# Agent attention and a squared-ReLU layer on one core: the step table that spaces the softmax chains of two query groups

## The chip, the cores and the metric

The kernel runs on one core of a Trainium2 chip. The metric is the device time of one execution in microseconds (us); the lower, the better. The kernel before was timed in three runs, with a median of 1907.89 us (1907.49 to 1918.07).

## The reference

Four batches of 12480 queries, keys and values of 128 channels, and 49 agents. The agents attend to the keys (`agent_v`), the queries attend to the agents, and the 49920 rows that come out go through a layer with a hidden width of 2048, all in float32:

```python
a2k = sm(agents, k)
agent_v = a2k @ v
q2a = sm(q, agents)
x = (q2a @ agent_v).reshape(B * S, D)
h = x @ w_in
r = np.maximum(h, 0.0)
return (r * r) @ w_out
```

`sm` is a softmax over scores scaled by 1/sqrt(128), with the maximum taken off.

## The kernel before

Since `agent_v` has only 49 rows, the kernel folds it into the weights of the layer: for each batch it makes `agent_v @ w_in` (49 x 2048) and multiplies the softmax of the queries, 49 wide, with it.

The query rows are cut into 49 groups of 1024. A group takes 16 *steps* of the main loop (784 in all), each for 512 rows and two of the 16 hidden blocks. Step i issues `mm1(i)` (6 matmuls at L440 into a PSUM tile `h`, of which there are two), `relu(i)` (ScalarE, L446, reads `h`), on every second step `square` (ScalarE, L449), `high` and `low` (VectorE, L453 and L457: the value split into two parts for fp32r matmuls), and `mm2` of a step 5 earlier (12 matmuls at L468 into one of two PSUM tiles `pair`). So mm1(i+2) needs relu(i) to have read its `h`. After 8 steps of mm2 `store` copies the sum out (ScalarE L473, VectorE L474) and writes 256 KB of the output (L475).

Beside this runs, for each group s, a chain that makes its softmax and lays it out with the 49 agents on the partitions:

- `q_load` (L313, 512 KB), then `q_scores` (matmuls L179) and `q_shift` (VectorE L333, L334, into buffer `e`), for two groups at once
- `q_exp` (ScalarE L337), `q_inverse` (VectorE L341 to L346), `q_norm` (GpSimd L349), `q_hi` (ScalarE L359) and `q_lo` (GpSimd L362), which leave `pp`, the softmax as two parts
- `q_turn` (L381): one transposing DMA from `pp` into `turned`, as 16-bit halves. Here it is called the *transpose*
- `q_sort` (L387): four DMAs that bring the lower and the upper halves into the two `planes`. The *sorts*
- `q_weave` (L392): two copies that put the halves together again in `woven`, one on ScalarE and one on GpSimd. The *joins*
- `q_spread` (L399): three DMAs, 1 MB in all, into `p_a` and `p_b`, which mm1 reads

There is one `pp` and one `planes`; `turned`, `woven` and the loaded tiles take turns in nine buffers. All DMAs are issued by SyncE's queue (SP), in program order: one that waits holds up those behind it. For the next batch a second chain runs: keys are loaded and scored (`k_load`, `k_scores`), the maximum is taken off (`k_sub`, GpSimd L214), `k_exp` (ScalarE L217), `v_load` and `v_acc` (matmuls L229).

The order on each engine is the program's. It comes from a list of (step, function) pairs, sorted by the step (L701): a fractional step number only sets the place in the order, nothing waits for a clock. `chain` (L494) finds for a row of functions the next free places on ScalarE, VectorE and TensorE. `plan_tokens(s, base)` (L531) calls it for one group; for an even s it also places the scores of s and s+1, and starts the softmax of s three steps behind them:

```python
first, base = chain(base, [("PE", q_scores, s, m), ("DVE", q_shift, s, m)])
...
base += 3
```

Of the kernel before, what the change touches and what calls it, by code (L numbers as in the profile page):

```python
# [25 lines left out]
def agent_attention_relu2_kernel(ctx: ExitStack, tc: tile.TileContext, qT, kT, v, agT, w_in, w_out, outT):  # L26
# [6 lines left out]
    nc = tc.nc  # L33
# [7 lines left out]
    NF = F // P  # L41
# [436 lines left out]
    LAG = 5  # L478
    steps = []

    def at(t, f, *args):
        steps.append((t, len(steps), f, args))
# [11 lines left out]
    def chain(t, todo):  # L494

        first = prev = None
        while todo:
            n = 1  # L500
            while todo[0][0] == "PE" and n < len(todo) and todo[n][1] in reads_bank and todo[n][0] != "PE":
                n += 1
            t += hop[prev][todo[0][0]] if prev else 0
            while True:
                g, p, ts = t, None, []
                for e, *_ in todo[:n]:
                    g += hop[p][e] if p else 0
                    while (e, g) in taken or (e == "PE" and g not in slots):
                        if p == "PE" and e == "DVE":
                            break  # L510
                        g += 1
                    ts.append(g)
                    p = e
                if todo[0][0] != "PE" or ts[-1] <= ts[0] + 1:
                    break
                t += 1
            for (e, f, *args), g in zip(todo, ts):
                soon = e == "DVE" and prev == "PE"
                if soon:
                    read.add(g)  # L520
                else:
                    taken.add((e, g))
                at(g + (.49 if soon and f is q_shift else .47 if soon else .45 if e == "PE" else .5), f, *args)
                prev = e
            first = ts[0] if first is None else first
            t, todo = ts[-1], todo[n:]
        return first, t
# [3 lines left out]
    def plan_tokens(s, base):  # L531
        todo = [("ACT", q_exp, s), ("DVE", q_inverse, s), ("POOL", q_norm, s), ("ACT", q_hi, s)]
        todo += [("POOL", q_lo, s)] + ([("PE", q_transpose, s), ("ACT", q_copy, s)] if s < 3 else [])
        if s > 1 and s % 2 == 0:
            m = min(2, NSG - s)
            first, base = chain(base, [("PE", q_scores, s, m), ("DVE", q_shift, s, m)])
            for x in range(s, s + m):
                at(first - 5, q_load, x)
            base += 3
        _, end = chain(base, todo)  # L540
        if s > 2:
            at(end + 1.9, q_turn, s)
            at(end + 3.9, q_sort, s)
            _, end = chain(end + 6, [("ACT", q_weave, s, 1, nc.scalar.copy)])
            at(end + .6, q_weave, s, 0, nc.gpsimd.tensor_copy)
        at(max(end + .9, (s - 1) * NF + .9), q_spread, s)
        assert end + 3 < s * NF, (s, end)

    def plan_batch(b, base):
# [128 lines left out]
    for y, x in enumerate((1.15, 1.16, 1.17)):  # L678
        at(x, w_first, 0, 4, 4, y, nc.vector)
    at(3.1, warm_rows, 6)  # L680
    plan_tokens(1, 3)
    for s in range(2, NSG):
        plan_tokens(s, (s - 2) * NF + NF // 2 + LAG - (0 if s < 3 else 8 if s % 2 else 3))
    t = 0
    for b in range(1, B):
        t = plan_batch(b, t)
# [41 lines left out]
```

## Time and profile before

| | us |
|---|---|
| median of three runs | 1907.89 |
| the profiled execution | 1912.69 |
| its span, first to last instruction | 1910.9 |
| TensorE busy | 1847.5 (97%) |
| ScalarE busy | 1676.3 (88%) |
| VectorE busy | 1670.2 (87%) |
| GpSimd busy | 388.3 (20%) |
| mean granted clock of TensorE | 0.989 |

The span leaves 1.8 us of the profiled execution outside. Engines in the rows: PE is TensorE's matmuls, PEld its weight loads, DVE VectorE, ACT ScalarE, POOL GpSimd, SP SyncE (SPq its queue of DMA issues). Busy time of PE overlaps from matmul to matmul, so a busy PE is not one at its full rate.

### The profile page before, as it was taken

The page shows a single profiled execution, that of the slowest core. Times are in us where ns is not written, and L with a number is a line of the kernel's source. Part 1 is how long each engine was busy: PE and PEld are TensorE (multiplying, and loading weights), DVE is VectorE, ACT ScalarE, POOL GpSimd, SP SyncE. Part 2 cuts the span into 40 slices and gives each one's busy share as a digit, 9 for nine tenths or more (in the row PEclk, how much of TensorE's full clock was granted, in tenths as well). Part 3 has the DMA queues.
Part 4 walks back from the last instruction along what each step waited for, and adds up shares of the span by engine and source line. Part 5 has one row for each costly group of instructions (what it writes and reads, how often), then busy time and mean ns, then how long its engine had stood idle before and what let it go on. Part 6 is the DMA issues. An engine that isn't in the chain of part 4 may idle for free.

```text
span 1910.9 us, 51820 instructions
## 1 busy us (share of the span) xinstructions
PE 1847.5 (97%) x23244; PEld 1482.4 (78%) x23244; DVE 1670.2 (87%) x1274; ACT 1676.3 (88%) x1535; POOL 388.3 (20%) x199
## 2 busy tenths in 40 slices
PE   9999999999999999999999999999999999999999
PEld 8688777787787877877788778777777787787787
DVE  7789897899888979989888899898888898898898
ACT  5788888898888979989888898899888998999997
POOL 1111232220201304213021142131220310210200
PEclk9999999999999999999999999999999999999999
DMA  9334432534434234244352342433522323323320
GB/s 383 111 90 126 121 88 92 139 87 145 127 102 122 75 105 118 82 120 115 116 156 82 97 113 82 120 101 92 143 65 71 95 77 86 95 64 99 95 70 21
DMA packets 158192, 204.75 MB, mean 107 GB/s; under 512 B 103408, under 2 KB 103664, under 8 KB 157970
## 3 DMA queue, kind: packets, MB, share of 16 engines
q1 hardware_dynamic: 157970, 201.44, 36.4%
q8 instruction: 182, 2.98, 0.6%
q14 instruction: 40, 0.33, 0.1%
HBM read 83.02 MB, written 25.56 MB: 57 GB/s over the span
## 4 chain that ended last, share of the span: by engine, by line
PE 50%; DMA 17%; ACT 11%; issue 7%; POOL 6%; DVE 5%; SPq 4%; ACTq 0%; POOLq 0%; DVEq 0%
PE pair L468 29%; PE h L440 16%; DMA turned<-pp 10%; ACT rg L446 6%; DMA planes<-turned 5%; SPq L387 3%; POOL pp L362 3%; PE pair L179 3%; ACT woven L392 2%; DVE gl L457 2%; POOL woven L392 2%; ACT rg L449 1%; DVE gh L453 1%; PE pair L229 1%; SPq L399 1%
## 5 line engine op out<-in xcount | busy, mean ns | idle before, releaser
L457 DVE TENSOR_TENSOR gl<-rg,gh 128x2048 fp32r<-128x2048 f32 x392 | 942.8, 2405 | 19.6 <-DVE gh L453 0.5
L446 ACT ACTIVATE rg<-h 128x1024 f32<-128x1024 f32 (+1 forms) x784 | 789.2, 1017 | 111.9 <-PE h L440 111.3
L449 ACT ACTIVATE rg<-rg 128x2048 f32<-128x2048 f32 x392 | 749.3, 1911 | 9.2
L453 DVE CAST gh<-rg 128x2048 fp32r<-128x2048 f32 x392 | 496.4, 1266 | 162.4 <-ACT rg L449 154.2
L468 PE MATMUL pair<-gh,wo_hi 64*128 64x512 f32 x3136 | 631.4, 393 | 1.5 <-issue 1.5
L468 PE MATMUL pair<-gh,wo_lo 64*128 64x512 f32 x3136 | 631.5, 393 | 0.0
L440 PE MATMUL h<-p_a,w_hi 49*128 49x512 f32 (+4 forms) x1616 | 509.6, 396 | 48.9 <-ACT rg L446 48.1
L440 PE MATMUL h<-p_b,w_hi 49*128 49x512 f32 (+4 forms) x1616 | 512.6, 396 | 1.7 <-DMA p_b<-w_lo 1.7
L468 PE MATMUL pair<-gl,wo_hi 64*128 64x512 f32 x3136 | 500.8, 393 | 1.8 <-DVE gl L457 1.7
L440 PEld LDWEIGHTS h<-p_a,w_hi 49*128 49x128 f32 x1616 | 287.0, 187 | 113.8 <-ACT rg L446 74.6
L468 PEld LDWEIGHTS pair<-gh,wo_lo 64*128 64x128 f32 x3136 | 310.6, 187 | 68.7
L468 PEld LDWEIGHTS pair<-gh,wo_hi 64*128 64x128 f32 x3136 | 309.1, 186 | 69.0 <-issue 1.7
L468 PEld LDWEIGHTS pair<-gl,wo_hi 64*128 64x128 f32 x3136 | 301.4, 185 | 72.2 <-DVE gl L457 6.9
L440 PE MATMUL h<-p_a,w_lo 49*128 49x512 f32 (+4 forms) x808 | 314.7, 389 | 0.0
L440 PE MATMUL h<-p_b,w_lo 49*128 49x512 f32 (+4 forms) x808 | 314.7, 389 | 0.0
L440 PEld LDWEIGHTS h<-p_b,w_hi 49*128 49x128 f32 x1616 | 289.6, 187 | 27.9 <-DMA p_b<-w_lo 2.0
L349 POOL TENSOR_TENSOR e<-e,sm 128x392 f32<-128x392 f32 x48 | 78.3, 1631 | 1020.6 <-DVE sm L346 906.6
L392 POOL COPY woven<-planes 128x1024 uint16<-128x1024 uint16 x46 | 125.8, 2735 | 253.8 <-DMA planes<-turned 189.4
L440 PEld LDWEIGHTS h<-p_a,w_lo 49*128 49x128 f32 x808 | 150.1, 186 | 29.0
L440 PEld LDWEIGHTS h<-p_b,w_lo 49*128 49x128 f32 x808 | 150.1, 186 | 1.7
L392 ACT COPY woven<-planes 128x1024 uint16<-128x1024 uint16 x46 | 62.8, 1366 | 75.1 <-DMA planes<-turned 65.5
L362 POOL TENSOR_TENSOR pp<-e,pp 128x392 fp32r<-128x392 f32 x48 | 99.4, 2071 | 114.5 <-ACT pp L359 114.5
(109 smaller groups left out, 858.9 us busy)
## 6 DMA issues: line engine op xcount, KB each, us to landing
vt<-v SPq DMA_DIRECT2D x52, 516.0 KB
qt<-qT SPq DMA_DIRECT2D x49, 512.0 KB
kt<-kT SPq DMA_DIRECT2D x52, 480.0 KB
outT<-ob SPq DMA_DIRECT2D x97, 256.0 KB
p_b<-woven SPq DMA_DIRECT2D x92, 256.0 KB
p_a<-woven SPq DMA_DIRECT2D x46, 512.0 KB
planes<-turned SPq DMA_DIRECT2D x184, 98.0 KB
raw<-w_in SPq DMA_DIRECT2D x4, 512.0 KB
```

Source lines behind the costliest of these rows:

```text
L179: nc.tensor.matmul(ps[r, u, c * A:(c + 1) * A], x[:, c, r], ag_sb[:, batch(c, r), :], start=True, stop=True)
L229: nc.tensor.matmul(ps[r], vt[:CH, c, r], piece(x)[:, c, :], start=x == n and c == 0, stop=x == n + m - 1 and c == G - 1)
L349: eng.tensor_tensor(out=es[s], in0=es[s], in1=sms.pop(s).to_broadcast([P, G, A]), op=ALU.mult)
L362: eng.tensor_tensor(out=halves(s)[1], in0=es.pop(s), in1=halves(s)[0].bitcast(F32), op=ALU.subtract)
L387: nc.sync.dma_start(out=to, in_=pss["t", s][w:2 * A:2, x])
L392: copy(PT["x"][:, :, :, w], planes[:, w])
L440: nc.tensor.matmul(h[:, u, x0:x1], w[ra[u], j, :], pt[u ^ lo][ra[u], x0:x1], start=x == 0, stop=x == 2)
L446: nc.scalar.activation(rgs[p][:, x], hs.pop(i)[:, :, :width(i)], AF.Relu)
L449: nc.scalar.activation(rgs[p], rgs[p], AF.Square)
L453: nc.vector.tensor_copy(ghs[p], rgs[p])
L457: nc.vector.tensor_tensor(out=gls[p], in0=rgs.pop(p), in1=ghs[p].bitcast(F32), op=ALU.subtract)
L468: nc.tensor.matmul(outs[t][u][:, :width(i)], w[rg[u], 2 * j + e, :], g[rg[u], e, :], start=j == 0 and x == 0, stop=j == NJ - 1 and x == 5)
```

## The change

Three numbers of the plan are moved.

```diff
         if s > 2:
-            at(end + 1.9, q_turn, s)
-            at(end + 3.9, q_sort, s)
-            _, end = chain(end + 6, [("ACT", q_weave, s, 1, nc.scalar.copy)])
+            at(end + 2.4, q_turn, s)
+            at(end + 4.9, q_sort, s)
+            _, end = chain(end + 8, [("ACT", q_weave, s, 1, nc.scalar.copy)])
             at(end + .6, q_weave, s, 0, nc.gpsimd.tensor_copy)
-        at(max(end + .9, (s - 1) * NF + .9), q_spread, s)
+        at(max(end + 1.4, (s - 1) * NF + .9) if s > 2 else end + .9, q_spread, s)
...
     for s in range(2, NSG):
-        plan_tokens(s, (s - 2) * NF + NF // 2 + LAG - (0 if s < 3 else 8 if s % 2 else 3))
+        plan_tokens(s, (s - 2) * NF + (13 if s < 3 else 7 if s % 2 else 6))
```

The places that come out are the same for all groups from 4 on (an odd group 3 too), in steps counted from step 16(s-2); an odd group's count begins 16 steps behind that of its even partner, and group s is first read at 32:

| | exp | norm | hi, lo | transpose | sorts | joins | spread |
|---|---|---|---|---|---|---|---|
| even s, before | 13.5 | 14.5 | 16.5 | 17.9 | 19.9 | 22.5 | 22.9 |
| even s, after | 9.5 | 10.5 | 13.5 | 15.4 | 17.9 | 21.5 | 22.4 |
| odd s, before | 5.5 | 6.5 | 8.5 | 9.9 | 11.9 | 14.5 | 16.9 |
| odd s, after | 7.5 | 8.5 | 10.5 | 12.4 | 14.9 | 18.5 | 19.4 |

The scores of a pair go from 10.45 to 6.45 of the even group's count. Stores stand at 4.2 and 12.2 of every 16. Some loads and matmuls of the key and value chain find other places a few steps away, since the places that they took are taken or free.

On SP's queue, from the transpose of group 16 to the load of groups 18 and 19, before (`turned<-pp` is a transpose, `planes<-turned` the sorts, `p_a` and `p_b<-woven` the spread, `outT<-ob` a store, `vt<-v` a load of values, `qt<-qT` one of queries):

```order
L381 DMA_TRANSPOSE turned_8943<-pp_90 128x16x128
L387 DMA planes_92<-turned_8943 49x1024 x4
L475 DMA outT<-ob_9014 128x512
L399 DMA p_b_9076<-woven_9071 64x1024 x2
L399 DMA p_a_9075<-woven_9071 128x1024
L221 DMA vt_9129<-v 128x1032
L221 DMA vt_9131<-v 128x1032
L381 DMA_TRANSPOSE turned_9159<-pp_90 128x16x128
L387 DMA planes_92<-turned_9159 49x1024 x4
L475 DMA outT<-ob_9231 128x512
L399 DMA p_b_9399<-woven_9348 64x1024 x2
L399 DMA p_a_9398<-woven_9348 128x1024
```

and the same place now:

```order
L381 DMA_TRANSPOSE turned_8890<-pp_90 128x16x128
L387 DMA planes_92<-turned_8890 49x1024 x4
L475 DMA outT<-ob_9014 128x512
L399 DMA p_b_9070<-woven_9040 64x1024 x2
L399 DMA p_a_9069<-woven_9040 128x1024
L221 DMA vt_9127<-v 128x1032
L221 DMA vt_9129<-v 128x1032
L475 DMA outT<-ob_9225 128x512
L381 DMA_TRANSPOSE turned_9231<-pp_90 128x16x128
L387 DMA planes_92<-turned_9231 49x1024 x4
L313 DMA qt_9395<-qT 128x1024
L313 DMA qt_9397<-qT 128x1024
```

The odd group's transpose (the second in each) stands right behind a store now, where it stood ahead of it, and the next pair's query loads stand right behind its sorts, ahead of its spread.

On GpSimd, from the first part of group 17's softmax (L349) to the joins of 16 and 17 (L392), before (`sk` at L214 is the key chain's k_sub, `pp` at L362 is q_lo):

```order
L349 TENSOR_TENSOR e_91<-e_91,sm_9041 128x392
L392 COPY woven_9071<-planes_92 128x1024
L214 TENSOR_TENSOR sk_99<-sk_99,mM_106 120x392
L362 TENSOR_TENSOR pp_90<-e_91,pp_90 128x8x49
L392 COPY woven_9348<-planes_92 128x1024
```

and now:

```order
L392 COPY woven_9040<-planes_92 128x1024
L214 TENSOR_TENSOR sk_99<-sk_99,mM_106 120x392
L349 TENSOR_TENSOR e_91<-e_91,sm_9095 128x392
L362 TENSOR_TENSOR pp_90<-e_91,pp_90 128x8x49
L214 TENSOR_TENSOR sk_99<-sk_99,mM_106 120x392
L392 COPY woven_9445<-planes_92 128x1024
```

Group 16's join stood between the two GpSimd operations of group 17's softmax; now it stands ahead of both.

## Rows read from the trace of the kernel before

**Rows 1.** Who waited for whom: us in total, times, longest us.

```profile
ACT woven L392 <- DMA planes<-turned: 65.5, 26, 7.3
PE h L440 <- ACT rg L446: 48.1, 44, 3.4
```

**Rows 2.** Timeline of ACT around the join of group 17: start us, us, instruction, idle before.

```profile
672.44 1.01 ACT L446 ACTIVATE rg<-h 128x1024 f32<-128x1024 f32 x1
679.31 1.34 ACT L392 COPY woven<-planes 128x1024 uint16<-128x1024 uint16 x1 [5.85 <-DMA planes<-turned]
```

**Rows 3.** Timeline of PE: the first matmul of steps 252, 254 and 257.

```profile
665.46 0.49 PE L440 MATMUL h<-p_a,w_hi 49*128 49x512 f32 x1 [0.40 <-ACT rg L446]
...
669.76 0.39 PE L440 MATMUL h<-p_a,w_hi 49*128 49x512 f32 x1
...
681.58 0.79 PE L440 MATMUL h<-p_a,w_hi 49*128 49x512 f32 x1 [3.41 <-ACT rg L446]
```

**Rows 4.** The chain that ended last, PE pieces: start us, us, what.

```profile
627.20 1.52 PE pair L179 x128
...
683.23 2.56 PE pair L468 x12
...
692.94 0.71 PE h L440 x6
693.65 1.40 PE pair L468 x12
```

**Rows 5.** Stretches: length, busy us (instructions) of PE, PEld, DVE, ACT, POOL, PEclk, DMA, GB/s.

```profile
602.00:612.00 10.00, 8.84 (x53) 7.07 (x55) 7.02 (x6) 8.91 (x9) 0.00 (x0) 0.66 0.38 105
...
1805.00:1812.00 7.00, 5.67 (x36) 4.57 (x38) 3.52 (x2) 6.94 (x7) 0.38 (x1) 0.76 0.55 152
```

**Rows 6.** Stretches: three periods of 32 steps in the last batch, and 60 us without a stall.

```profile
1573.83:1791.15 217.32, 209.92 (x2116) 167.04 (x2114) 192.92 (x133) 198.99 (x175) 34.97 (x18) 0.99 0.32 85
...
1595.00:1655.00 60.00, 60.00 (x630) 48.23 (x630) 56.75 (x41) 57.11 (x52) 9.32 (x5) 1.00 0.30 74
```

**Rows 7.** Timeline of POOL from group 17's norm to its q_lo.

```profile
655.21 1.65 POOL L349 TENSOR_TENSOR e<-e,sm 128x392 f32<-128x392 f32 x1 [10.68 <-ACT rg L446]
656.80 3.43 POOL L392 COPY woven<-planes 128x1024 uint16<-128x1024 uint16 x1
660.15 1.98 POOL L214 TENSOR_TENSOR sk<-sk,mM 120x392 f32<-120x392 f32 x1
662.09 3.00 POOL L362 TENSOR_TENSOR pp<-e,pp 128x392 fp32r<-128x392 f32 x1
```

**Rows 8.** Timeline of SP's issues, the same stretch: the us are those of the issue.

```profile
660.26 1.18 SPq L399 DMA_DIRECT2D p_b<-woven  x2
...
662.11 2.26 SPq L221 DMA_DIRECT2D vt<-v  x2
665.12 4.98 SPq L381 DMA_TRANSPOSE turned<-pp  x1
673.54 3.07 SPq L387 DMA_DIRECT2D planes<-turned  x4
676.72 0.39 SPq L475 DMA_DIRECT2D outT<-ob  x1
```

**Rows 9.** The chain that ended last, group 14's transfers: start us, us, what.

```profile
568.36 4.29 DMA turned<-pp
...
575.05 3.44 DMA planes<-turned
```

**Rows 10.** The same view, the last sort of group 13.

```profile
516.99 4.30 DMA planes<-turned
```

**Rows 11.** Timeline of SP, the issues behind group 13's sorts.

```profile
517.79 0.40 SPq L475 DMA_DIRECT2D outT<-ob  x1
518.24 1.11 SPq L174 DMA_DIRECT2D kt<-kT  x2
```

**Rows 12.** Timeline of DVE: the addition of the store at step 252.

```profile
670.10 0.68 DVE L474 TENSOR_TENSOR ob<-ob,pair 128x512 f32<-128x512 f32 x1
```

## The prediction

> **What bounds the kernel now.** I read the waits first, then the timeline of one long wait, then the stretches by engine.
>
> The waits name one pair [rows 1]: ScalarE stood 65.5 us at its joining copy because the sorts had not landed, and TensorE stood 48.1 us at mm1 because a relu came late. The timeline shows that these are one thing. ScalarE finishes a relu at 673.45 and begins the join at 679.31, after 5.85 us of waiting [rows 2]. The relus behind it in ScalarE's order are late by as much, mm1 has two `h` tiles and soon lacks a free one, and step 257 waits 3.41 us [rows 3]. So a wait on ScalarE reached TensorE with about 0.6 to 0.7 of its length (3.41/5.85, 48.1/65.5).
>
> A long wait costs twice. In the undisturbed stretch 6 matmuls of mm1 take 0.71 and 12 of mm2 1.40 us, 2.10 for a step; behind the stall the same 12 take 2.56 [rows 4]. [...] There are seven such stretches. (1 - clock) x length is 3.4 us in two of them (0.34 x 10) and 1.7 in five (0.24 x 7): 15.3 us.
>
> Without a stall TensorE is busy for all of 60 us and ScalarE for 57.1 of them [rows 6]. So TensorE bounds the kernel and ScalarE has 5% to spare: little, but it keeps pace there.
>
> The losses thus add up to 48.1 + 15.3 = 63.4 us. Idle time undercounts, since ends of matmuls are modelled; three whole periods show by how much. 96 steps between the transposes of groups 41 and 47 took 217.32 us; 96 x 2.10 plus three pairs of scores at 1.52 [rows 4] make 206.2, so 11.1 were lost, where idle time (217.32 - 209.92 = 7.4) and one clock stretch (1.7) tell 9.1 [rows 6]. At that ratio, 1.22, the whole is 77 us. I take 70 as what there is to win.
>
> Why the joins wait is in GpSimd's and SP's order, shown best at group 17. Its norm (655.21) is ahead of group 16's join, which runs from 656.80 and delays group 17's q_lo to 662.09 + 3.00 = 665.09 [rows 7]. The spread of group 16 can go only after that join, at 660.26, two value loads follow at 662.11, and the transpose of 17 is issued at 665.12 behind 2 MB of them: its sorts start 8.4 us later [rows 8], against 4.3 for a transpose with nothing ahead [rows 9].
>
> **The change part by part.** No instruction is added or removed; all durations stay. What changes is the distance between a chain's links, in steps of 2.10 us.
>
> *Distance from q_lo to the join:* six steps before, eight now, in every group: 4.2 us more for the transfers. They need, from the transpose's issue, 4.29 to its landing, 2.4 for the first three sorts, 3.44 for the last to land [rows 9]: 10.1 us. The longest single wait was 7.3 us [rows 1], so distance alone leaves at most 3.1 of it.
>
> *Even groups:* q_lo stands at step 13.5. It needs q_hi, which ScalarE reaches 3.7 us or less after the step's start, and takes 2 to 3 us [rows 7]: I take 5.5 to 6.5 us after the start of step 13. The halves then lie ready at 15.6 to 16.6 us. ScalarE comes to the join 3.7 us after the start of the join's step (673.45 against step 254 at 669.76 [rows 2, 3]), here 8 x 2.10 + 3.7 = 20.5. Four us are spare: no wait.
>
> *Odd groups:* on GpSimd the even join now goes ahead of the odd norm, and the even spread and the loads are issued some six steps (12.6 us) before the odd transpose instead of 3 to 5 us. So the 8.4 us should fall to 4.3. But the odd transpose is now behind the store of step 12. SP must wait for that addition: 670.10 + 0.68 against step 252's start at 665.46, 5.3 us [rows 12, 3], which is later than q_lo (step 10, 4.2 us earlier, plus 6). Then 10.1 us of transfers, and one more price: the next pair's query loads (1 MB) are issued right behind the sorts. Group 13 had a store and key loads there [rows 11], and its last sort took 4.30 instead of 3.44 [rows 10, 9]: 0.9. Ready at 5.3 + 10.1 + 0.9 = 16.3 us after step 12's start. ScalarE comes to the join at step 18: 6 x 2.10 + 3.7 = 16.3 us. The spare time is nil where TensorE has nothing extra in these six steps (15 of the 23 odd groups), and 1.5 us where a key score or `v_acc` lies in them (8). With an error of 0.8 us either way, those 15 wait about 0.45 us on average, 0.7 of which arrives at TensorE: 5 us in all, and too short to bring the clock down.
>
> *The store itself* puts 256 KB into the same DMA queue just ahead of the transpose. The trace has no such pair. From one side it costs nothing (no gain, as it adds work); from the other, 2 MB ahead cost 8.4 - 4.3 = 4.1 us [rows 8, 9]. I take an eighth, 0.5, by bytes: it lies inside the error above; 4.1 is kept for the range.
>
> [...]
>
> *The scores' move* to step 6.45 puts them two steps behind a store that empties the same PSUM tile. The store's addition ends 5.3 us after step 4's start; TensorE comes to the scores after the third step, 6.3. One us is spare. Their query loads, now behind the odd sorts, leave SP 5.3 + 4.3 + 3.1 = 12.7 us after the odd step 12 and are wanted at step 22, 21 us: they have 8 us to land.
>
> *Lost cover:* an earlier spread or a later one costs nothing; group s is first read at step 32 and the latest spread is at 22.4.
>
> The sum: 70 of losses less 5 that stay makes 65. Against its own time that is 1912.7 - 65 = 1848 for a profiled execution; the median of the runs shown lies 4.8 lower, so 1907.9 - 65 = **1843 us**.
>
> **The rivals.**
>
> *The odd waits stay (A).* If the store costs the transpose the full 4.1 us, ScalarE waits 16.3 + 4.1 - 16.3, about 4 us, in 15 odd groups and 2.5 in 8: 80 us, of which 0.7 or 56 reach TensorE, with little clock loss. Then 1907.9 - 70 + 56 = 1894. For it: zero spare time and the order on SP. Against: bytes.
>
> *ScalarE becomes the bound (B).* Without stalls there is no point at which lateness is wiped out, and ScalarE has 2.9 us spare in 60 [rows 6]. At the joins it gets 1.34 (join), then a store copy and an exponential within two to three steps. If each of 46 joins costs TensorE 0.5 us, 23 us stay: 1866. Against: the even joins stood as close to a store before, most without a wait.
>
> *GpSimd stands in front of the odd softmax (C), slower.* Place: the even join, now ahead of the odd norm, blocks GpSimd until the even sorts have landed; q_hi on ScalarE waits for the norm. The join should end near 16.6 + 3.4 = 20 us after the start of the even step 13, a k_sub behind it at 22, and the norm is wanted when the odd scores' sums are there, 11 steps and 3 us (26 us) after it; q_hi has 2 more. It decides from 6 us of lateness on; group 17's transpose was 4.1 us late. To eat 65 us, each of 23 odd groups must be late by 6 us and cost TensorE 3 us beyond that: 1907.9 - 65 + 69 = 1912 or above. Nothing in the rows shows even transfers so late.
>
> *It does nothing (D).* The waits move with the join, because the later transpose eats the distance in both kinds of group: 1900 to 1908. The even groups' four spare us speak against it.
>
> **How the numbers follow.** Forecast 0.73, A 0.11, B 0.08, D 0.04, C 0.04. The forecast's own range is 1907.9 - 77 = 1831 to 1858 (losses 63, 13 left). With B and half of A the range is 1829 to 1876. About 1% (19 us) is what a measurement of this kernel can tell from no change; faster by more than that (under 1889) are the forecast, B and about half of A, 0.90; within it D and some of A, 0.06; slower 0.04.
>
> **What would show it right or wrong.** Right: ScalarE's wait for the sorts falls from 65.5 us to under 10, TensorE's for the relu from 48.1 to under 10; the mean granted clock rises from 0.989 to about 0.997, since (1 - 0.989) x 1910.9 = 21 us, of which 15.3 go; odd transposes take 4 to 5 us, and SP holds them for the store's addition and no longer for q_lo. A shows as odd transposes of 6 us and more with joins that wait. B shows as waits of TensorE for relus with no wait of ScalarE ahead. C shows as waits of q_hi (L359) on GpSimd. The forecast is wrong if the joins no longer wait and the time still stays over 1876.

## The result, and the profile after

The changed kernel takes 1850.59 us (median of four runs, 1849.86 to 1854.21), the kernel before 1909.66 beside it (four runs, 1907.49 to 1918.07). The ratio is 0.9687, with a 95% interval of 0.9654 to 0.9719: 59 us less, of a forecast 65. The predicted 1843.0 is 7.6 us too low, and the range of 1829 to 1876 holds the result.

The waits of after, all engines, that answer to [rows 1] (us in total, times, longest us):

```profile
ACT woven L392 <- DMA planes<-turned: 5.9, 6, 1.8
...
ACT woven L392 <- issue: 4.8, 5, 1.8
...
PE pair L179 <- issue: 4.2, 2, 3.6
...
PE h L440 <- ACT rg L446: 3.6, 7, 0.8
...
PE pair L468 <- issue: 2.9, 2, 2.5
...
PE pair L229 <- issue: 1.8, 3, 0.9
```

Before, ScalarE waited 75.1 us at the joins: 65.5 put down to the sorts [rows 1] and 9.6 with nothing named. Now the same two rows of L392 make 10.7. TensorE's waits for relus fell from 48.1 us [rows 1] to 3.6. The three "issue" rows of PE are what the prediction doesn't have: TensorE stood 8.9 us with nothing in the profile to wait for (here and below, single waits of 0.2 us and less are left out). In the kernel before there were two such rows, 1.5 us each; they stand here behind its "issue" row of the joins:

```profile
ACT woven L392 <- issue: 9.6, 5, 4.4
...
PE pair L468 <- issue: 1.5, 1, 1.5
PE pair L229 <- issue: 1.5, 1, 1.5
```

Span and granted clock of after; before it was 1910.9 us at 0.989:

```profile
core 0: 1852.4 us, clock 0.996
```

The chain that ended last, by engine, of before and then of after (share of the span):

```profile
PE 50%; DMA 17%; ACT 11%; issue 7%; POOL 6%; DVE 5%; SPq 4%; ACTq 0%; POOLq 0%; DVEq 0%
```

```profile
PE 77%; DVE 7%; ACT 6%; issue 5%; DMA 4%; SPq 1%; POOL 0%; ACTq 0%; DVEq 0%; POOLq 0%
```

The transfers and GpSimd, 23% of the chain together, are down to 4%: the joins no longer hold the end.

Group 17 once more, the place of [rows 7, 8]. Timeline of SP (start us, us of the issue):

```profile
636.67 1.17 SPq L399 DMA_DIRECT2D p_b<-woven  x2
...
638.55 2.32 SPq L221 DMA_DIRECT2D vt<-v  x2
654.00 0.34 SPq L475 DMA_DIRECT2D outT<-ob  x1
654.44 2.23 SPq L381 DMA_TRANSPOSE turned<-pp  x1
660.12 3.07 SPq L387 DMA_DIRECT2D planes<-turned  x4
663.23 0.93 SPq L313 DMA_DIRECT2D qt<-qT  x2
```

Timeline of GpSimd, the same stretch:

```profile
630.89 3.10 POOL L392 COPY woven<-planes 128x1024 uint16<-128x1024 uint16 x1 [5.50 <-DMA planes<-turned]
...
643.01 1.66 POOL L349 TENSOR_TENSOR e<-e,sm 128x392 f32<-128x392 f32 x1 [7.13 <-DVE sm L346]
647.88 0.97 POOL L362 TENSOR_TENSOR pp<-e,pp 128x392 fp32r<-128x392 f32 x1 [3.20 <-ACT pp L359]
```

VectorE's addition for that store, and ScalarE's join:

```profile
653.29 0.68 DVE L474 TENSOR_TENSOR ob<-ob,pair 128x512 f32<-128x512 f32 x1
```

```profile
666.09 1.37 ACT L392 COPY woven<-planes 128x1024 uint16<-128x1024 uint16 x1 [1.02 <-issue]
```

The even spread and the value loads are issued 16 to 18 us ahead of the odd transpose now. q_lo ends at 648.85, the transpose is issued at 654.44: SP held it 5.6 us for the addition that ends at 653.97. Its sorts start 5.7 us after it, where they started 8.4 us after it before. Here ScalarE comes 1.0 us early; before it was 5.85 [rows 2].

### The profile page after: what moved, and what is told of

It is laid out like the page before. It is cut to its first block, busy times and chain, and to the rows that moved or that the text cites. A ratio compares the mean times of both kernels' runs of the same rounds, so it can differ in the third digit from the quotient of the medians.

```text
span 1852.4 us, 51847 instructions
## 1 busy us (share of the span) xinstructions
PE 1826.9 (99%) x23244; PEld 1488.1 (80%) x23244; DVE 1682.6 (91%) x1274; ACT 1676.3 (90%) x1535; POOL 368.3 (20%) x199
## 4 chain that ended last, share of the span: by engine, by line
PE 77%; DVE 7%; ACT 6%; issue 5%; DMA 4%; SPq 1%; POOL 0%; ACTq 0%; DVEq 0%; POOLq 0%
PE pair L468 47%; PE h L440 25%; PE pair L179 3%; ACT rg L446 3%; DVE gl L457 2%; DVE gh L453 2%; DMA turned<-pp 2%; PE pair L229 1%; ACT rg L449 1%; DMA planes<-turned 1%; SPq L387 1%; ACT woven L392 1%; DMA raw<-w_in 1%; DMA vt<-v 1%; DVE ob L474 0%
## 5 line engine op out<-in xcount | busy, mean ns | idle before, releaser
L457 DVE TENSOR_TENSOR gl<-rg,gh 128x2048 fp32r<-128x2048 f32 x392 | 942.7, 2405 | 17.9
L453 DVE CAST gh<-rg 128x2048 fp32r<-128x2048 f32 x392 | 516.9, 1319 | 100.0 <-ACT rg L449 88.1
L440 PE MATMUL h<-p_b,w_hi 49*128 49x512 f32 (+4 forms) x1616 | 505.8, 391 | 0.9 <-DMA p_b<-w_lo 0.9
L440 PE MATMUL h<-p_a,w_hi 49*128 49x512 f32 (+4 forms) x1616 | 499.1, 391 | 4.4 <-ACT rg L446 3.6
L468 PEld LDWEIGHTS pair<-gh,wo_lo 64*128 64x128 f32 x3136 | 314.7, 186 | 70.7 <-issue 3.8
L349 POOL TENSOR_TENSOR e<-e,sm 128x392 f32<-128x392 f32 x48 | 76.5, 1595 | 660.8 <-DVE sm L346 585.9
L392 POOL COPY woven<-planes 128x1024 uint16<-128x1024 uint16 x46 | 95.7, 2081 | 496.4 <-DMA planes<-turned 421.1
L362 POOL TENSOR_TENSOR pp<-e,pp 128x392 fp32r<-128x392 f32 x48 | 94.7, 1973 | 196.6 <-ACT pp L359 196.6
L214 POOL TENSOR_TENSOR sk<-sk,mM 120x392 f32<-120x392 f32 x39 | 94.8, 2430 | 17.9 <-DVE mM L211 17.9
```

Of the source, the lines that this page charges most:

```text
L214: eng.tensor_tensor(out=piece(n), in0=piece(n), in1=m.rearrange("p (o a) -> p o a", o=1).to_broadcast([CH, G, A]), op=ALU.subtract)
L349: eng.tensor_tensor(out=es[s], in0=es[s], in1=sms.pop(s).to_broadcast([P, G, A]), op=ALU.mult)
L362: eng.tensor_tensor(out=halves(s)[1], in0=es.pop(s), in1=halves(s)[0].bitcast(F32), op=ALU.subtract)
L392: copy(PT["x"][:, :, :, w], planes[:, w])
L440: nc.tensor.matmul(h[:, u, x0:x1], w[ra[u], j, :], pt[u ^ lo][ra[u], x0:x1], start=x == 0, stop=x == 2)
L453: nc.vector.tensor_copy(ghs[p], rgs[p])
```

## The experiments

A batch of runs has its own chip and its own runs of the kernel before, so kernels of different batches are compared by their ratio to it. The diffs are against the changed kernel.

**1. The distances alone.** The softmax starts where it did before; the joins keep the new distance.

```diff
-        plan_tokens(s, (s - 2) * NF + (13 if s < 3 else 7 if s % 2 else 6))
+        plan_tokens(s, (s - 2) * NF + (13 if s < 3 else 5 if s % 2 else 10))
```

> The changed kernel with the starts of before (10 for even, 5 for odd groups) and only the longer distances. Theory (both halves of the change count): GpSimd again takes the odd norm ahead of the even join, so the odd q_lo ends late and the odd transpose stands right behind the even spread, 7 to 8 us long; but the join stands 8 steps behind q_lo. The two about cancel: ScalarE waits 10 to 25 us at the joins, all in odd groups, and the time is 1850 to 1870. Rival 1 (standing apart is what counts): as before, 1895 to 1910, ScalarE's wait 40 us or more. Rival 2 (distance alone counts): as the changed kernel, 1848 to 1853, ScalarE's wait 6 us.

Measured: 1841.88 us (1840.67 to 1843.70), ratio 0.9636 (0.9615 to 0.9656). That is below the expectation, nearest to its rival 2, and no slower than the whole change (the intervals just touch). Waits of ScalarE and PE in this run, then SP's issues around the transpose of group 17:

```profile
ACT woven L392 <- DMA planes<-turned: 5.9, 4, 2.4
...
PE h L440 <- ACT rg L446: 2.6, 2, 2.0
```

```profile
642.32 1.19 SPq L399 DMA_DIRECT2D p_b<-woven  x2
...
645.21 4.01 SPq L381 DMA_TRANSPOSE turned<-pp  x1
651.47 0.36 SPq L475 DMA_DIRECT2D outT<-ob  x1
652.52 3.94 SPq L387 DMA_DIRECT2D planes<-turned  x4
```

The odd transpose is still behind the even spread and takes 7.3 us to its sorts, and it doesn't matter: it is issued ahead of the store, as soon as q_lo is done, and the longer distance holds all of it. The chains need not stand apart for the gain.

**2. The starts alone.** The distances and the spread's place go back.

```diff
-            at(end + 2.4, q_turn, s)
-            at(end + 4.9, q_sort, s)
-            _, end = chain(end + 8, [("ACT", q_weave, s, 1, nc.scalar.copy)])
+            at(end + 1.9, q_turn, s)
+            at(end + 3.9, q_sort, s)
+            _, end = chain(end + 6, [("ACT", q_weave, s, 1, nc.scalar.copy)])
...
-        at(max(end + 1.4, (s - 1) * NF + .9) if s > 2 else end + .9, q_spread, s)
+        at(max(end + .9, (s - 1) * NF + .9), q_spread, s)
```

> The changed kernel with the distances of before (transpose 1.9, sorts 3.9, join 6 steps behind q_lo) and only the new starts (6 and 7). Theory: the transposes take 4 to 5 us in both kinds of group, ready 16 us after the step of q_lo where ScalarE comes at 16.3: no spare time in 46 groups, ScalarE waits 15 to 30 us in all, time 1855 to 1880. Rival 1 (standing apart is what counts): as the changed kernel, 1848 to 1853. Rival 2 (distance alone counts): 1890 to 1910.

Measured: 1854.37 us (1850.17 to 1855.59), ratio 0.9698 (0.9678 to 0.9717), just under what was expected; ScalarE waits 14.3 us for the sorts, TensorE 9.0 for relus. Each half alone gives nearly the whole gain, so they don't add up: either the joins are moved back, or the transfers are freed of what stands ahead of them. In this kernel too the odd transpose is ahead of the store, and most of the waiting is at even joins (ten of 23, 11.7 us), which stand two steps closer to their q_lo than in the change.

**3. The odd transpose ahead of the store.**

```diff
-            at(end + 2.4, q_turn, s)
+            at(end + (2.1 if s % 2 else 2.4), q_turn, s)
```

> The changed kernel with the odd transpose 2.1 instead of 2.4 steps behind q_lo, which puts it ahead of the store of step 12 on SP's queue and moves nothing else. Theory (the store's addition holds the odd transpose): odd transposes are issued some 3 to 5 us earlier, ScalarE's wait for the sorts falls from 5.9 us to under 1.5, time 1 to 4 us lower, 1847 to 1850. Rival (the odd waits come from the loads on the DMA engines, not from the store): ScalarE's wait stays at 4 to 7 us, time the same within 1 us.

Measured: 1840.92 us (1839.57 to 1842.48), ratio 0.9632 (0.9615 to 0.9648): 10 us below the change, more than expected. SP's issues for group 17:

```profile
645.08 2.23 SPq L381 DMA_TRANSPOSE turned<-pp  x1
650.20 0.34 SPq L475 DMA_DIRECT2D outT<-ob  x1
650.64 3.53 SPq L387 DMA_DIRECT2D planes<-turned  x4
```

None of ScalarE's 46 joins waits any more (0.0 us of idle time ahead of them). In the spans (1852.4 and 1838.3, 14.1 less) the parts are: relus 3.6 to 0.6, "issue" waits of TensorE 8.9 to 3.4, and (1 - clock) x span from 7.4 to 1.8, together 14.1. The sum is that close by luck, since the clock is given to 0.001 and each of its two losses is good to 0.9 us only. So more than a third of the difference is in waits that have no releaser, which the next two runs look at; why they should shrink with this exchange is not shown.

**4. The query loads earlier**, away from the pile of transfers ahead of the longest of these waits.

```diff
-                at(first - 5, q_load, x)
+                at(first - 12 if s > 2 else first - 5, q_load, x)
```

> The changed kernel with the query loads 12 instead of 5 steps ahead of their scores: on SP's queue they come ahead of the odd transpose instead of behind its sorts. Order on TensorE unchanged. Theory (TensorE's two longest waits, 2.47 us at 526.8 and 3.62 us at 1266.2, inside or just behind a run of 128 narrow matmuls, are for its own instructions, whose fetch comes late while the DMA engines work off 3 MB of loads and spread): with 1 MB less in that pile both fall below 1 us and the clock no longer drops there: 8 to 11 us less, 1840 to 1844. Rival 1 (TensorE waits there for query data): it goes too, but only at 1266; the one at 526.8, behind key scores, stays: 1844 to 1847. Rival 2 (the place in the instruction stream alone decides): both stay, 1849 to 1852.

Measured: 1847.32 us (1845.62 to 1848.27), ratio 0.9664 (0.9648 to 0.9680); the interval overlaps that of the change, and the expected 1840 to 1844 is missed. The wait of 3.62 us near 1266 is gone, the one of 2.47 near 527 stays, and another grew from 0.56 to 2.16 us, at a run of narrow matmuls where the query loads, issued at 335.35, now join a pile of value loads and spread. That run on TensorE's timeline in the change, and in this experiment:

```profile
343.28 1.56 PE L229 MATMUL pair<-sk,vt 120*32 120x49 f32 x121
345.39 0.29 PE L229 MATMUL pair<-sk,vt 120*32 120x49 f32 x7 [0.56 <-issue]
```

```profile
341.88 1.56 PE L229 MATMUL pair<-sk,vt 120*32 120x49 f32 x121
345.60 0.29 PE L229 MATMUL pair<-sk,vt 120*32 120x49 f32 x7 [2.16 <-issue]
```

So two of these three waits changed along with the transfers in flight: over 335 to 343 the DMA engines moved 317 GB/s here and 259 in the change, and ahead of 1266 they were busy 0.72 of 10 us here (from 1255) and 1.01 in the change (from 1257). The place stays the same, after matmul 121 of 128, in both kernels. One wait gone and one that stays is also what rival 1 said (TensorE waits for query data near 1266); run 5 settles that.

**5. TensorE's instructions shifted by 32.** 16 of the 24 warming matmuls on constant data at the start are left out; nothing reads their results.

```diff
-    at(Z, warm_up, 12)
+    at(Z, warm_up, 4)
```

> The changed kernel with 16 matmuls fewer in the warm-up at the very start, so that everything that TensorE does later stands 32 instructions earlier in its stream; order, loads and steps unchanged. Theory (TensorE's waits without a releaser come where its instructions are fetched in blocks of 256, a block ends in the last 30 or so of the 256 instructions of a score run, and the DMA engines are over 0.8 busy): the five runs that end a block there now (near 344, 732, 1087, 1121 and 1266 us) end it some 20 instructions after their start instead, and wait under 0.3 us; in their place come only runs with a DMA share under 0.75 ahead of them. These waits, 8.9 us now, fall below 3.5 us, the clock drop at 1266 goes, time 5 to 10 us lower, 1841 to 1846. Rival (the loads alone decide): the waits stay where they are, time 1849 to 1852.

Measured: 1848.42 us (1845.25 to 1851.59), ratio 0.9670 (0.9653 to 0.9686). The five places at which runs of narrow matmuls stalled in the change no longer do, with the same transfers around them: the place of the waits goes with the number of TensorE's instructions. The query loads near 1266 stand where they stood, and their scores run through; the wait is now behind them, in mm2, so it isn't for query data:

```profile
1262.31 1.59 PE L179 MATMUL pair<-ag_sb,qt 128*32 128x49 f32 x128
...
1266.37 0.50 PE L468 MATMUL pair<-gh,wo_hi 64*128 64x512 f32 x1 [0.88 <-issue]
```

"issue" waits fall from 8.9 to 3.7 us, the clock rises to 0.998. The profiled span is 4.7 us shorter than that of the change, but the median isn't measurably lower and the expected 1841 to 1846 is missed: ScalarE's joins wait 12.6 us in this execution instead of 10.7, and TensorE 7.1 us for relus instead of 3.6. So it seems that a part of what TensorE won it lost again at the joins, which have no time to spare; one execution of each doesn't show more.

**6. Runs 3 and 5 together.**

> Both of the last two: odd transpose ahead of the store, and the stream 32 instructions earlier. Theory: no join waits, and of the 3.6 us of waits without a releaser left there less than 2 stay: 1836 to 1840. Rival (the loads alone decide): as with the transpose alone, 1840 to 1842.

Measured: 1837.01 us (five runs, 1835.32 to 1838.71), ratio 0.9608 (0.9595 to 0.9622), as expected. No wait at the joins, 1.6 us of "issue" waits. It is the fastest here, and faster than both kernels; against run 3 alone the intervals overlap a little. Some 0.7 us of it may be the shorter start (the first mm1 is at 53.9 instead of 54.6 us).

**7. The odd joins one step earlier** (17.5 instead of 18.5; the even ones keep their place). The odd spread goes with them, and a few key and value loads find other places.

```diff
-            _, end = chain(end + 8, [("ACT", q_weave, s, 1, nc.scalar.copy)])
+            _, end = chain(end + 7, [("ACT", q_weave, s, 1, nc.scalar.copy)])
```

> The changed kernel with the join 7 instead of 8 steps behind q_lo. Only the odd joins move (17.5 instead of 18.5); the even ones find the same place. Theory (an odd join has no time to spare where TensorE has nothing extra): 15 odd groups lose 2.1 us and wait about 2.5 us each, 8 wait about 0.6 us; ScalarE waits 35 to 48 us, 0.7 of which reach TensorE: time 1870 to 1885. Rival (the spare time is larger than that sum says, since the halves land earlier): ScalarE waits under 20 us, time 1850 to 1862.

Measured: 1936.46 us (1931.75 to 1939.92), ratio 1.0128 (1.0107 to 1.0150): slower than the kernel before, and far beyond the expected 1870 to 1885. Its waits, and one odd group on SP:

```profile
ACT woven L392 <- DMA planes<-turned: 69.2, 22, 4.9
...
PE h L440 <- ACT rg L446: 60.2, 24, 4.5
...
ACT woven L392 <- DMA qt<-qT: 4.8, 1, 4.8
```

```profile
1599.64 0.34 SPq L475 DMA_DIRECT2D outT<-ob  x1
1600.08 2.27 SPq L381 DMA_TRANSPOSE turned<-pp  x1
1605.13 3.06 SPq L387 DMA_DIRECT2D planes<-turned  x4
```

The store's addition still releases the transpose, and the join now comes 2.1 us sooner. The mechanism is the expected one, with three prices higher. All 23 odd joins wait, 74.0 us with the one put down to a query load, where 35 to 48 were expected; the runs don't show why a step of 2.1 us costs them 63 us, 2.75 each. Of that 60.2/74.0 = 0.81 reaches TensorE, not 0.6 to 0.7. And the granted clock is 0.978 over a span of 1938.1 us: (1 - clock) x span is 42.6 us, against 7.4 in the change: 35 us more lost in clock, on top of 56.6 more us of waits for relus.

**8. Run 1 with the odd transpose behind the store.**

```diff
-            at(end + 2.4, q_turn, s)
+            at(end + (3.4 if s % 2 else 2.4), q_turn, s)
...
-        plan_tokens(s, (s - 2) * NF + (13 if s < 3 else 7 if s % 2 else 6))
+        plan_tokens(s, (s - 2) * NF + (13 if s < 3 else 5 if s % 2 else 10))
```

> The longer distances alone (starts of before), with the odd transpose moved one step back (3.4 instead of 2.4 behind q_lo), which puts it behind the store of step 12 and leaves the odd join where it is, 5 steps behind that store. Theory (what decides is the time from the release of the odd transpose to the join, and the store's addition is that release): same 5 steps as with the join at 7 behind the changed starts, so the odd joins wait some 60 to 80 us in all and the clock drops: 1915 to 1945, slower than before. Rival (distance from q_lo to the join decides, 8 steps are enough): 1840 to 1850, like the longer distances alone.

Measured: 1926.06 us (1922.81 to 1928.66), ratio 1.0075 (1.0058 to 1.0092), as expected; the clock is 0.984. Its waits:

```profile
ACT woven L392 <- DMA planes<-turned: 65.7, 21, 4.0
...
PE h L440 <- ACT rg L446: 53.6, 23, 3.8
```

The odd transposes are shorter than in run 1 (median 4.5 instead of 6.7 us to the first sort) and the joins wait all the same: it is the later start that makes them wait, not the length.

**9. Run 7 with the odd transpose ahead of the store.**

```diff
-            at(end + 2.4, q_turn, s)
+            at(end + (2.1 if s % 2 else 2.4), q_turn, s)
...
-            _, end = chain(end + 8, [("ACT", q_weave, s, 1, nc.scalar.copy)])
+            _, end = chain(end + 7, [("ACT", q_weave, s, 1, nc.scalar.copy)])
```

> The changed kernel with the join at 7 steps (1936 us) and the odd transpose 2.1 steps behind q_lo, ahead of the store. Theory: the transposes go 3 to 5 us earlier, which is more than the 2.1 us that the join at 7 took away; ScalarE's wait at the joins falls from 69 us to under 15: 1842 to 1852. Rival (7 steps are too few wherever the transpose stands): 1900 or more.

Measured: 1840.76 us (1838.21 to 1841.38), ratio 0.9622 (0.9608 to 0.9636), just under what was expected. ScalarE's joins wait 2.6 us in all, where they waited 74.0; then SP's issues for one odd group:

```profile
ACT woven L392 <- DMA qt<-qT: 1.7, 1, 1.7
...
ACT woven L392 <- DMA planes<-turned: 0.9, 1, 0.9
```

```profile
1517.01 1.73 SPq L381 DMA_TRANSPOSE turned<-pp  x1
1520.89 0.34 SPq L475 DMA_DIRECT2D outT<-ob  x1
1521.33 3.07 SPq L387 DMA_DIRECT2D planes<-turned  x4
```

Runs 7 and 9 differ in one exchange on SP's queue, transpose and store of each odd group, with all else in the same order, and that is worth (1.0128 - 0.9622) x 1911 = 97 us; runs 8 and 1 differ in the same, in 22 of the 23 groups, 84 us. This settles what decides for the odd groups: the time from the transpose's release to the join. Ahead of the store the release is q_lo, behind it the store's addition.

## Why the prediction was right, and what it missed

*What bounded the kernel.* Right: with the joins' waits gone the relu waits and the clock's losses go too. The 70 us that it took to be there to win were, if anything, few: run 6 is 1911.24 - 1837.01 = 74 us below its kernel before, near the upper figure of 77 that came from scaling by 1.22; some 1.4 of the 74 are fewer waits of TensorE without a releaser (3.0 to 1.6). The clock's 15.3 us among these losses are, in the trace of before, seven stretches granted 0.50 between 370 and 1811 us, two of 6.8 us and five of 3.4: 0.66 over 10 us and 0.76 over 7 [rows 5] come to that.

*Even groups, 4 us spare, no wait.* Right: none of the 23 even joins waits. Run 2, which takes 4.2 us from them, makes ten of them wait, so four us is about the size.

*Odd transposes from 8.4 to about 4.3 us, held by the addition.* Right for most: from the transpose's issue to the first sort it is 4.3 to 4.8 us in 18 of the 23 odd groups, and 5.2 to 6.2 in five (group 17 is one of them), for which the runs have no cause. The 8.4 was group 17's: before, the 23 odd transposes took 4.3 to 9.9 us, median 6.9, and six of them under 4.5 already. The hold shows in every odd group: the transpose is issued 0.5 us behind the end of the store's addition (0.8 in one) and 2.4 to 5.7 us behind that of q_lo. In run 3 it follows q_lo within 0.1 us in all 23.

*The store ahead of the transpose, 0.5 us by its bytes, 4.1 at most.* The low end holds: 4.3 to 4.8 in those 18 groups, all behind a store, against 4.29 with nothing ahead [rows 9]. So the store costs them 0.5 us at most. The five longer ones need no store: in run 3, without one just ahead, nine odd transposes take 5.0 to 6.2 us. What the store does cost is SP's wait ahead of it, 5.6 us at group 17. The prediction had that wait in its sum; it didn't see that a plan without it (run 3) would be 10 us faster, about half of that in the waits told of below.

*Spare time nil in the odd groups.* Right in kind: 11 of 23 odd joins wait, up to 1.8 us, 10.7 in all. TensorE got 3.6 of that, a third; of the short waits most is absorbed, of the long ones little (0.81 reaches TensorE in run 7). A single share of 0.7 for both was too simple, and the 5 us came out near the 3.6 by luck: the two errors, too little waiting (6.75, 15 x 0.45) and too high a share, go against each other.

*The scores' move, the spread, the even join ahead of the odd norm.* Right at nothing: TensorE has no wait for the query loads, and GpSimd's even joins end 9 us ahead of the odd norm (630.89 + 3.10 and 643.01 at groups 16 and 17). Rival C has no trace; B would show as relu waits with no wait of ScalarE ahead, and only 3.6 us of relu waits are left.

*Rival A* did not happen in the change, but run 7 shows the state that it described, brought about by an earlier join and not by a dear store. Its 56 us of relu waits came almost exactly (56.6 more than in the change), though from 74.0 x 0.81 and not 80 x 0.7, which is luck. The part of it that fails is "with little clock loss", which was 35 us. In the chances, 0.90 for a time under 1889 counts most of A; with the half that is named it is 0.865.

*The step that fell short: "70 of losses less 5 that stay makes 65".* It counts what goes and the joins that stay, and nothing new. The profiled execution was to take 1848 us; its span is 1852.4, with the 1.8 outside 1854.2, so 6.2 are missing. The trace has them in three terms: TensorE's waits without a releaser, 8.9 us instead of 3.0, so 5.9; the clock, (1 - 0.996) x 1852.4 = 7.4 where the predicted 0.997 gives 5.5, so 1.9; less 1.4 at the relus. That is 6.4. The stretches of 5 us behind the two longest waits, one of which is shown (length, busy us of PE, PEld, DVE, ACT, POOL, PEclk, DMA share, GB/s), were granted 0.66 each, the one behind the other from 530: 0.34 x 5 x 2 = 3.4 us of the 7.4.

```profile
1270.00:1275.00 5.00, 5.00 (x35) 3.97 (x32) 3.40 (x4) 3.63 (x3) 0.00 (x0) 0.66 0.02 5
```

The terms thus add up for one execution, with 0.9 us of rounding in the clock and the 70 taken as right, which was itself a choice between 63.4 and 77. That the time falls by as much when these waits alone are taken away is not shown. Runs 4 and 5 took some of them away, and their intervals overlap that of the change.

## What to carry to other kernels

Count the distance between chained transfers from what really releases the first of them, and that includes the instruction ahead of it in its in-order queue: here one exchange with a store that waits for an addition was worth 84 to 97 us, and 10 where the join stood a step later. A plan whose waits come out at just zero can be a step away from a loss larger than the gain (59 us won by the change, 84 lost from there to run 7), since there the idling was paid a second time in the clock (35 us in run 7); after such a change, try the next smaller distance to see how near the edge is. And look for waits of TensorE without a releaser where narrow matmuls run beside a pile of transfers: here they came to 8.9 us.

## What the runs showed of the hardware

The change has seven waits of TensorE over 0.3 us without a releaser, 8.9 us in all. That TensorE waited there for its own instructions is inferred from the counts below; no row names it. The longest, on TensorE's timeline in the change, is inside a run of 128 equal matmuls, which no semaphore parts:

```profile
1264.61 1.57 PE L179 MATMUL pair<-ag_sb,qt 128*32 128x49 f32 x123
1269.80 0.28 PE L179 MATMUL pair<-ag_sb,qt 128*32 128x49 f32 x5 [3.62 <-issue]
```

Ahead of it SP issued 3 MB within 6 us, and the 16 DMA engines were busy all the time, a share of 1.01 (SP's issues, and the stretch by engine):

```profile
1254.54 0.94 SPq L313 DMA_DIRECT2D qt<-qT  x2
1255.53 0.92 SPq L221 DMA_DIRECT2D vt<-v  x2
1258.59 1.17 SPq L399 DMA_DIRECT2D p_b<-woven  x2
1259.80 0.77 SPq L399 DMA_DIRECT2D p_a<-woven  x1
```

```profile
1257.00:1267.00 10.00, 8.78 (x185) 6.67 (x181) 8.56 (x6) 9.62 (x9) 1.37 (x1) 1.00 1.01 282
```

The page's list of DMA queues has two of a kind called instruction (packets, MB, share of 16 engines):

```profile
q8 instruction: 182, 2.98, 0.7%
q14 instruction: 41, 0.34, 0.1%
```

The 182 packets of the first are 16 KB each. Spread over TensorE's 2 x 23244 matmuls and weight loads they make 255.4 instructions a packet, or 256.2 with the 141 of its stream that only wait: 64 bytes an instruction, by this division. That they are TensorE's is read from this count alone. All seven waits in the change and both in the kernel before stand at the same remainder, 193, when TensorE's instructions, those that only wait too, are counted from the start and divided by 256; the 256 instructions from one such place to the next are called a block here. So do all 27 in the nine other runs, run 5 included, whose stream is 32 shorter from the start. A packet of this queue starts at 1267.30, as the load of the DMA engines ends (their busy share is 0.95 from 1266 to 1267 and 0.32 from 1268 to 1269), and TensorE goes on at 1269.80, 2.5 us later; at the other long wait it is 526.88 and 529.31, 2.4 us. A run of 128 narrow matmuls and their weight loads, 256 instructions, passes in 1.6 us, less than those 2.4 and 2.5; so, by the same inference, a packet that starts late isn't there in time. Of the runs whose block ends near their own end (from instruction 242 of 256 on) the five with the DMA engines over 0.8 busy in the 4 us ahead stalled, for 0.34 to 3.62 us, and the three with 0.2 or less did not; one that ends its block at 234, with 0.95, did not either.

The other two waits, one of them the 2.47 us, stand in mm2, behind narrow runs. What all seven have in common is a short block ahead: 85 to 127 of its 128 matmuls are narrow, and it passed in 2.5 to 7.0 us, where the median block takes 10. Taken in order, the packets fit the blocks one to one: a packet starts between 2.7 us ahead and 4.6 us behind the start of one block, and the next block starts 2.27 us after the packet at the least. The seven waits are among the nine places where this distance is shortest (2.27 to 2.51 us). Run 4 moves the transfers, and the wait of 3.62 us is gone; run 5 moves the instructions, the five waits inside narrow runs are gone, and 3.7 us are left where 8.9 were.

Of the 182 blocks 175 are crossed without such a wait. Ahead of the seven others short blocks and busy DMA engines meet: the engines' share in the 4 us before the packet is 0.87 to 1.02. What isn't settled is why some short blocks beside busy DMA engines pass without a wait, as the one with 0.95 did.
